# A shorter offset between the first two blocks of a fused attention and mixture-of-experts kernel, with the second block's attention moved into the first three slots

## The chip, the cores and the metric

The kernel runs on one core of a Trainium2 chip. The metric is the device time of one execution in microseconds (us). Three runs of the kernel before took 1556.98, 1557.83 and 1558.25 us; the median is 1557.83 us.

## The reference

Three stages follow one another. The matrices of the second stage come as 64-bit floats; everything else is float32.

```python
# attention: q, k, v are (8, 8, 576, 64); keys and values are averaged over groups of 8
k_p = k.reshape(B, H, Sp, pool, D).mean(axis=3)
v_p = v.reshape(B, H, Sp, pool, D).mean(axis=3)
attn = softmax(scale * np.matmul(q, k_p.transpose(0, 1, 3, 2)))
x = np.matmul(attn, v_p) ...                      # (4608, 512)
# dense layer: w_in is (512, 2048), w_out is (2048, 512)
h = x @ w_in
x = np.maximum(0.01 * h, h) @ w_out
# eight experts, the best one for each token, w1 is (512, 1024), w2 is (1024, 512)
logits = x @ w_gate
out[mask] = gate_w[mask, None] * (np.maximum(x[mask] @ w1[e], 0.0) @ w2[e])
```

## The kernel before, in words

**Precision.** TensorE works on operands split into a high and a low part; a product takes three matmuls (high by high, high by low, low by high). So each weight, each activation and each attention result is first split: ScalarE (ACT) copies the high part, VectorE (DVE) subtracts it to get the low part. Most ACT copies go through the helper `act_copy` (L129) and most DVE subtractions through `sub` (L132), so their lines in the profile are those of the helpers.

**Blocks and slots.** The 4608 tokens are worked on in 18 blocks of 256. The dense layer's 2048 inner columns are 16 pieces `f` of 128. A **slot** is one pair (block b, piece f). Its steps are `g1` (12 matmuls of 128x256 at L498, an ACT copy with factor 0.01, the DVE maximum at L506), `g_hi` and `g_lo` (the split of the result) and, two slots later, `g2` (six matmuls of 128x512 at L526). The list `seq` holds the slots in order. Blocks 0 and 1 are interleaved: block 1 follows block 0 by `LAG` pieces. With `LAG = 4` slots 0 to 3 are pieces 0 to 3 of block 0; then the two blocks alternate; slots 28 to 31 are the last four pieces of block 1. From slot 32 on, one block after the other follows.

**Weights of the dense layer.** In the opening each 64-bit piece of `w_in` (kind 0) and `w_out` (kind 1) must be turned into two float32r parts. `w_conv1` does the first half on a piece: two ACT activations (L463, L464) and four DVE operations (L465, L468, L471, L474). `w_conv2` does the second: an ACT copy and a DVE subtraction. The function `conv` calls them within a slot:

```python
def conv(s, b, f):
    f += LAG * b
    kinds = (b,) if s > LAG and f < NF else (0, 1) if b == 0 else ()
    # w_conv2 for piece f + 1 and w_conv1 for piece f + 2, for each kind in kinds
```

Up to slot `LAG` a slot of block 0 converts both kinds; after that a slot of block 0 converts `w_in` and a slot of block 1 `w_out`. Each slot of block 0 needs its `w_in` piece for `g1`.

**Order of the work.** Every engine executes its own instructions in the order in which the program issues them. Within a slot the loop issues: `g1`; `g_lo` of the slot before; the hooks of this slot (`run_slot`); `g2` of the slot two back; `conv`; `g_hi`. Hooks are functions tied to a slot number by `at(slot, fn, ...)`.

**Attention.** A token tile of 128 rows takes five steps: `att_a` (four TensorE transposes of q at L359, an ACT copy `qT`), `att_b` (eight score matmuls at L378 in two banks; for each bank a DVE maximum at L384 and a subtraction), `att_e` (ACT exponential, L390), `att_n` (DVE row sum, reciprocal and scaling, L394 to L399) and `att_c` (transposes at L410 and L416, ACT copies, DVE subtractions into `at_t` and `rm_t`). When both tiles of a block are through, `att_av` multiplies by the values (16 matmuls at L437 in two banks), and ACT and DVE split the result into the block's input (`x_t`, for block 1 `x1`, printed as `x`). All of these take their PSUM bank from `pt("att")`, which hands out two banks in turn, so a step can start writing only after the step two banks back has been read. Tiles 0 and 1 (block 0) are done ahead of slot 0. Tiles 2 and 3 (block 1) are hooks of slots 0 to 3, and block 1's `att_av` is a hook of slot `LAG`. The hooks of later tiles, of the pooled keys and values of the second sequence (`kvn_k`, `kvn_v`, `kvn_r` at slots 6 to 16) and of the expert weights stand at fixed slot numbers.

Of the kernel before, what the change touches and what calls it, by code (L numbers as in the profile page):

```python
# [21 lines left out]
def kernel(  # L22
# [14 lines left out]
    B, H, S, D = q.shape  # L37
    NT, DM = out.shape
    DFF = moe_w_in.shape[1]
    LAG = 4  # L40
    E, _, FE = moe2_w1.shape
    POOL = 8
    SP = S // POOL
# [953 lines left out]
    seq = []  # L997
    for i in range(NF + LAG):
        if i < NF:
            seq.append((0, i))  # L1000
        if i >= LAG:
            seq.append((1, i - LAG))
    seq += [(b, f) for b in range(2, NB) for f in range(NF)]
# [3 lines left out]
    def at(slot, fn, *a):  # L1007
        hooks.setdefault(slot, []).append((fn, a))

    def plan():  # L1010
        for t in range(4, NT // P):
            b, i = divmod(t, TPB)
            s = (b - 1) * NF + 1 + 7 * i
            at(s - 1, att_a, t)
            if t + 1 < NT // P:
                at(s - 1, q_load, t + 1)
            at(s + 1, att_b, t)
            at(s + 2, att_e, t)
            at(s + 3, att_n, t)
            at(s + 5, att_c, t)  # L1020
        for b in range(2, NB):
            at((b - 1) * NF + NF - 1, att_av, b)
        for nb in range(2, B):
            t = S * nb // P
            b, i = divmod(t, TPB)
            sb_ = (b - 1) * NF + 2 + 7 * i
            use = []
            c = sb_ - 1
            while len(use) < 4:
                if c % NF in (1, 3, 5, 8, 10, 12, 14) and (not use or use[0] - c >= 3):  # L1030
                    use.insert(0, c)
                c -= 1
            use += [use[3] + 2, use[3] + 4, use[3] + 6]
            for i in range(7):
                at(use[i], kv_use, nb, i)
                if i + 2 < 7:
                    at(use[i], kv_load, nb, i + 2)
                at(use[i] - 2 + (i > 3), kv_pool, nb, i)
            at(max(use[0] - 6, 0), kv_load, nb, 0)
            at(use[0] - 5, kv_load, nb, 1)  # L1040
        for i in range(E * NCH):
            s = 34 + i * 9 // 5
            at(s, ps_load, i)
            at(s + 2, ps_split, i)
            at(s + 3, ps_store, i)
        for b in range(NB - 1):
            s = (b + 1) * NF + 1
            lg_at = []
            if b == 0:
                at(30, y_evac, 0)  # L1050
                at(31, y_tr, 0, 0)
                at(32, y_tr, 0, 1)
                at(33, y_logit, 0)
                r = (34, 36)
            elif b == 1:
                ev, r = 37, (46, 48)
                lg_at = [38 + j // 2 for j in range(16)]
            elif b == NB - 2:
                ev, r = None, (s + 9, s + 11)
                lg_at = [s + j // 2 for j in range(16)]  # L1060
            else:
                ev, r = None, (s + 15, s + 19)
                lg_at = [s + max(j - 1, 0) for j in range(16)]
            if b == 1:
                at(ev, y_evac, b)
            for j, x in enumerate(lg_at):
                at(x, logit, b, j)
            at(r[0], route_a, b)
            at(r[1], route_b, b)
            at(r[1], route_c, b, 0)  # L1070
            at(r[1] + 2, route_c, b, 1)
# [34 lines left out]
    with tc.manual_schedule():  # L1106
# [66 lines left out]
            at(6 + 2 * i, kvn_k, 1, i)  # L1173
        at(14, kvn_v, 1)
        at(16, kvn_r, 1)
        for fn, t, o in zip((att_a, att_b, att_e, att_n, att_c) * 2, (2,) * 5 + (3,) * 5, (0, 0, 1, 1, 2, 1, 1, 2, 2, 3)):
            at(o, fn, t)
        at(LAG, att_av, 1)
        at(31, prefill)
        at(36, step_consts)  # L1180
        at(20, lambda: nc.sync.dma_start(out=wgk, in_=moe2_w_gate.rearrange("(k p) e -> p k e", p=P)))
        at(27, gate_rows)
        at(4, q_load, 4)
        plan()
        pend = []
# [4 lines that stand above are left out]
            for kind in kinds:  # L1190
                if (kind, f + 1) in w_mid:
                    w_conv2(kind, f + 1)
                    if w_todo:
                        w_load64()
            for kind in kinds:
                if (kind, f + 2) in w_raw:
                    w_conv1(kind, f + 2)
# [171 lines left out]
```

## Time and profile before

| | |
|---|---|
| median of three runs | 1557.83 us |
| profiled execution, its own time | 1558.05 us |
| its span, first to last instruction | 1556.0 us |
| TensorE matmuls busy (PE) | 1472.8 us, 95% |
| VectorE busy (DVE) | 939.4 us, 60% |
| ScalarE busy (ACT) | 626.8 us, 40% |
| mean granted TensorE clock | 0.975 |

Busy shares are averages over stages with different limits, so a change in one stage has to be read from that stage's own stretch. The opening, slots 0 to 31, lies between about 36 and 197 us of the span. Times in the rows are microseconds from the span's start.

### The profile page before, as it was taken

What the parts mean: (1) busy time and instruction counts of PE and PEld (TensorE: products, weight loads), DVE (VectorE), ACT (ScalarE), POOL (GpSimd) and SP (SyncE); (2) the same over time, 40 slices, a digit from 0 to 9 for tenths busy, and PEclk for the clock granted to TensorE, in tenths of its full rate; (3) what the DMA queues carried; (4) which work ended last, traced back from release to release, by engine and by line L of the source; (5) the groups of instructions that cost most, each with busy time, mean ns of one, the idle gap of its engine ahead of it and who ended that gap; (6) DMA issues with size and microseconds to landing.
All of it is one profiled execution on the core that took longest, in us unless ns stands there. A gap on an engine that the chain in (4) does not pass through costs nothing. (4 is left out here: it accounts for less than half of the span.)

```text
span 1556.0 us, 25769 instructions
## 1 busy us (share of the span) xinstructions
PE 1472.8 (95%) x9272; PEld 1317.6 (85%) x9272; DVE 939.4 (60%) x2468; ACT 626.8 (40%) x1442; POOL 327.3 (21%) x294
## 2 busy tenths in 40 slices
PE   3698989999999999999999999999799999999998
PEld 3586879999898888899989989988699999998887
DVE  6998658879778878877877977664122121211111
ACT  4676434544444454444444444322122222222222
POOL 4000012232232233222222332121212111111111
PEclk8699999999999999999999999999899999999999
DMA  9443135555544545535645644143511117566160
GB/s 216 148 132 100 63 99 190 167 188 169 169 167 166 182 149 185 184 140 171 197 153 157 203 149 163 48 178 122 245 41 55 35 48 300 211 257 259 41 250 24
DMA packets 121386, 238.06 MB, mean 153 GB/s; under 512 B 56845, under 2 KB 65041, under 8 KB 117544
## 3 DMA queue, kind: packets, MB, share of 16 engines
q1 hardware_dynamic: 90312, 139.81, 28.7%
q10 hardware_dynamic: 23328, 76.56, 13.0%
q0 software_dynamic: 7616, 20.01, 3.8%
q8 instruction: 75, 1.23, 0.3%
q14 instruction: 55, 0.45, 0.1%
HBM read 317.78 MB, written 87.38 MB: 260 GB/s over the span
## 5 line engine op out<-in xcount | busy, mean ns | idle before, releaser
L526 PE MATMUL y<-w,ghl 128*128 128x512 f32 x1728 | 466.3, 406 | 2.8 <-DVE ghl L132 2.5
L526 PEld LDWEIGHTS y<-w,ghl 128*128 128x128 f32 x1728 | 310.1, 192 | 61.7 <-DVE ghl L132 6.3
L132 POOL TENSOR_TENSOR ps<-ps 128x512 f32<-128x512 f32 x128 | 181.6, 1419 | 482.2 <-ACT ps L129 361.8
L498 PEld LDWEIGHTS h<-x_t,w 128*128 128x128 f32 x1776 | 239.6, 195 | 39.8 <-DVE w L132 16.9
L498 PE MATMUL h<-x_t,w 128*128 128x256 f32 x1776 | 246.4, 288 | 24.0 <-DVE w L132 15.3
L546 DVE CUSTOM_DVE_ANT_0 junk<-y,wg 128x512 bf16<-128x512 f32 x256 | 200.3, 783 | 1.9
L498 PEld LDWEIGHTS y<-x_t,w 128*128 128x128 f32 x1488 | 193.2, 189 | 9.6
L498 PE MATMUL y<-x_t,w 128*128 128x256 f32 x1488 | 196.1, 282 | 0.0
L935 PE MATMUL y<-w,ghl 128*128 128x512 f32 x672 | 176.5, 401 | 0.9 <-DVE ghl L923 0.9
L935 PEld LDWEIGHTS y<-w,ghl 128*128 128x128 f32 x672 | 120.4, 190 | 22.4 <-DVE ghl L923 1.3
L129 ACT ACTIVATE g<-h 128x256 f32<-128x256 f32 x164 | 63.0, 384 | 145.9 <-PE h L498 132.8
L991 POOL DMA_INDIRECT out_dram<-kv,sidx x40 | 40.1, 1003 | 382.5 <-ACT kv L990 199.3
L923 DVE SCALAR_TENSOR_TENSOR ghl<-h,ghl 128x256 fp32r<-128x256 f32 x56 | 23.8, 425 | 135.9 <-ACT ghl L922 135.9
L506 DVE TENSOR_TENSOR h<-g,h 128x256 f32<-128x256 f32 x132 | 56.0, 424 | 77.7 <-ACT g L129 77.2
L132 DVE TENSOR_TENSOR at_t<-a,at_t 128x512 fp32r<-128x512 f32 x62 | 42.7, 688 | 87.6 <-ACT at_t L129 87.2
L129 ACT ACTIVATE ghl<-h 128x256 fp32r<-128x256 f32 x132 | 50.7, 384 | 92.9 <-PE y L526 42.8
L129 ACT ACTIVATE ps<-ps 128x512 fp32r<-128x512 f32 x128 | 80.5, 629 | 17.8 <-DMA ps<-in_moe_w_dram 8.7
L129 ACT ACTIVATE ghl<-y 128x256 fp32r<-128x256 f32 x124 | 47.3, 382 | 95.2 <-DVE y L506 50.5
L132 DVE TENSOR_TENSOR x_t<-a,x_t 128x512 fp32r<-128x512 f32 x60 | 41.1, 688 | 51.7 <-ACT x_t L129 51.7
L129 ACT ACTIVATE g<-y 128x256 f32<-128x256 f32 x124 | 47.4, 382 | 60.9 <-PE y L498 53.4
L295 DVE TENSOR_TENSOR kv<-kv 72x512 f32<-72x512 f32 (+8 forms) x126 | 68.0, 540 | 3.2
L613 POOL DMA_INDIRECT lst<-ent,six x36 | 37.8, 1051 | 150.4 <-DVE six L612 115.1
(291 smaller groups left out, 2157.2 us busy)
## 6 DMA issues: line engine op xcount, KB each, us to landing
w<-wsp SPq DMA_DIRECT2D x108, 2048.0 KB
wsp<-ps ACTq DMA_DIRECT2D x128, 512.0 KB
ps<-in_moe_w_dram SPq DMA_DIRECT2D x128, 256.0 KB
y_d<-y ACTq DMA_DIRECT2D x18, 512.0 KB
q<-in_q_dram SPq DMA_DIRECT2D x28, 256.0 KB
kv<-in_k_dram SPq DMA_DIRECT2D x24, 288.0 KB
kv<-in_v_dram SPq DMA_DIRECT2D x24, 256.0 KB
ps<-in_moe_w_in_dram SPq DMA_DIRECT2D x8, 512.0 KB
```

Of the source, the lines that this page charges most:

```text
L129: nc.scalar.activation(o, i, AF.Copy, scale=scale)
L132: eng.tensor_tensor(out=o, in0=a, in1=b, op=ALU.subtract)
L295: eng.tensor_tensor(out=o, in0=t[:, :, 0:w], in1=t[:, :, w:2 * w], op=ALU.add)
L498: nc.tensor.matmul(p[:, 0:BLK], win(f)[:, kk, l], xv[:, kk, r], start=(n == 0), stop=(n == 3 * KD - 1))
L506: nc.vector.tensor_tensor(out=g, in0=t, in1=h, op=ALU.max)
L526: nc.tensor.matmul(y_ps[b, i], hl[:, l, i * P:i * P + P], wout(f)[:, r], start=(f == 0 and l + r == 0), stop=(last and l == 1),)
L546: nc.vector.tensor_tensor_reduce(out=jk, in0=y_sb[b][:, i], in1=wg_t[0][:, e], scale=1.0, scalar=0.0, op0=ALU.mult, op1=ALU.add, accum_out ...
L613: nc.gpsimd.indirect_dma_start(out=lst, out_offset=bass.IndirectOffsetOnAxis(ap=ix[:, 0:1], axis=0), in_=ent[:, i, :], in_offset=None, bou ...
L923: nc.vector.scalar_tensor_tensor(out=hl[:, 1], in0=b, scalar=0.0, in1=f32(hl[:, 0]), op0=ALU.max, op1=ALU.subtract)
L935: nc.tensor.matmul(o_ps[2 * p + i], hl[:, l, i * P:i * P + P], w[:, r], start=(f == 0 and l + r == 0), stop=(f == 7 and l == 1),)
L991: nc.gpsimd.indirect_dma_start(out=out, out_offset=bass.IndirectOffsetOnAxis(ap=sidx[:, t:t + 1], axis=0), in_=o, in_offset=None, bounds_c ...
```

## The change

`LAG` becomes 2. Slots 0 to 2 are then pieces 0 to 2 of block 0, the two blocks alternate from slot 3 to slot 28, and slots 29 to 31 are the last pieces of block 1; there are still 32 slots. `conv` converts both kinds in slots 0, 1 and 2 instead of 0 to 4, nothing in slot 3, and one kind per slot from slot 4 on. The attention steps of tiles 2 and 3 and of block 1's `att_av` get new slots. The evacuation and the logits of block 0 move on by one slot each.

```diff
-    LAG = 4
+    LAG = 2
...
             if b == 0:
-                at(30, y_evac, 0)
-                at(31, y_tr, 0, 0)
-                at(32, y_tr, 0, 1)
-                at(33, y_logit, 0)
-                r = (34, 36)
+                at(31, y_evac, 0)
+                at(32, y_tr, 0, 0)
+                at(33, y_tr, 0, 1)
+                at(34, y_logit, 0)
+                r = (35, 37)
...
-        for fn, t, o in zip((att_a, att_b, att_e, att_n, att_c) * 2, (2,) * 5 + (3,) * 5, (0, 0, 1, 1, 2, 1, 1, 2, 2, 3)):
+        for fn, t, o in zip((att_a, att_b, att_e, att_n, att_c) * 2, (2,) * 5 + (3,) * 5, (0, 0, 0, 1, 1, 1, 1, 1, 2, 2)):
             at(o, fn, t)
         at(LAG, att_av, 1)
```

**ACT in slot 0.** `g<-h` is the activation of `g1`, `qT` the query of tile 2, `pr<-pr` its exponential, `w<-ps` and `w<-y` are the high parts of `w_conv2`, the L463 and L464 rows belong to `w_conv1`. Before:

```order
L129 ACTIVATE g<-h_362 128x256
L129 ACTIVATE qT<-a_378 128x512
L129 ACTIVATE w_301<-ps 128x4x128
L129 ACTIVATE w_332<-y_113 128x512
L463 ACTIVATE junk<-r_114 128x512
L464 ACTIVATE e_107<-junk,ebias 128x512
```

and with the change:

```order
L129 ACTIVATE g<-h_362 128x256
L129 ACTIVATE qT<-a_378 128x512
L390 ACTIVATE pr<-pr 128x576
L129 ACTIVATE w_301<-ps 128x4x128
L129 ACTIVATE w_332<-y_113 128x512
L463 ACTIVATE junk<-r_114 128x512
L464 ACTIVATE e_107<-junk,ebias 128x512
```

The exponential of tile 2 has moved from slot 1 to slot 0, ahead of the copies and activations of the weight conversion.

**DVE in slot 1.** Rows L394 to L399 are `att_n` of tile 2, `w_118<-a` are the two banks of `att_b` of tile 3, `w_301<-r_114` is the first subtraction of `w_conv2`. Before:

```order
L394 TENSOR_REDUCE st<-pr 128x8
L395 TENSOR_SCALAR st<-st 128x8
L396 RECIPROCAL st<-st 128x8
L399 TENSOR_TENSOR pn<-pr,st 128x512
L399 TENSOR_TENSOR pn<-pr,st 128x64
L384 TENSOR_REDUCE w_118<-a_447 128x4
L132 TENSOR_TENSOR w_118<-a_447,w_118 128x288
L384 TENSOR_REDUCE w_118<-a_452 128x4
L132 TENSOR_TENSOR w_118<-a_452,w_118 128x288
L132 TENSOR_TENSOR w_301<-r_114,w_301 128x4x128
```

and with the change:

```order
L394 TENSOR_REDUCE st<-pr 128x8
L395 TENSOR_SCALAR st<-st 128x8
L396 RECIPROCAL st<-st 128x8
L399 TENSOR_TENSOR pn<-pr,st 128x512
L399 TENSOR_TENSOR pn<-pr,st 128x64
L132 TENSOR_TENSOR at_t<-a_441,at_t 128x4x128
L132 TENSOR_TENSOR rm_t<-a_448,rm_t 32x2x128
L384 TENSOR_REDUCE w_118<-a_460 128x4
L132 TENSOR_TENSOR w_118<-a_460,w_118 128x288
L384 TENSOR_REDUCE w_118<-a_465 128x4
L132 TENSOR_TENSOR w_118<-a_465,w_118 128x288
L132 TENSOR_TENSOR w_301<-r_114,w_301 128x4x128
```

The two subtractions of `att_c` for tile 2, which use the transposed output of `att_n`, now follow `att_n` at once; before they stood in slot 2.

**DVE in slot 2, with the change.** `w_118` is tile 3, `x_104` the input of block 1:

```order
L399 TENSOR_TENSOR w_118<-w_118 128x512
L399 TENSOR_TENSOR w_118<-w_118 128x64
L132 TENSOR_TENSOR at_t<-a_513,at_t 128x4x128
L132 TENSOR_TENSOR rm_t<-a_520,rm_t 32x2x128
L132 TENSOR_TENSOR x_104<-a_526,x_104 128x2x256
L132 TENSOR_TENSOR x_104<-a_537,x_104 128x2x256
L132 TENSOR_TENSOR w_301<-kv,w_301 128x4x128
```

`att_n`, `att_c` and `att_av` stand one behind the other; before they were in slots 2, 3 and 4 with conversions of weights between them.

## Rows read from the trace of the kernel before

**Rows 1.** The page: busy time and share of the span of each engine, and the granted TensorE clock in 40 equal slices, in tenths.

```profile
PE 1472.8 (95%) x9272; PEld 1317.6 (85%) x9272; DVE 939.4 (60%) x2468; ACT 626.8 (40%) x1442; POOL 327.3 (21%) x294
...
PEclk8699999999999999999999999999899999999999
```

**Rows 2.** Busy time by stretch: the stretch, its length, busy us (and instructions) of PE, weight loads, DVE, ACT, POOL, then the granted clock, DMA share, GB/s. They are slot 1, slot 2, slot 3 and slots 5 to 24, each cut where DVE begins a slot's maximum.

```profile
51.80:62.40 10.60, 6.77 (x27) 5.97 (x27) 10.22 (x23) 6.11 (x12) 0.00 (x0) 0.50 0.29 99
62.40:72.45 10.05, 6.46 (x25) 5.41 (x25) 9.68 (x21) 6.21 (x12) 0.00 (x0) 0.67 0.31 104
...
72.45:80.51 8.06, 5.74 (x37) 4.86 (x36) 7.79 (x15) 5.83 (x10) 0.00 (x0) 0.98 0.51 149
...
88.62:172.04 83.42, 73.32 (x424) 60.53 (x424) 75.69 (x148) 56.07 (x116) 0.69 (x3) 0.94 0.29 89
```

**Rows 3.** Whom DVE waited for between 26 and 172 us: total us, times, longest us.

```profile
DVE e L465 <- ACT e L464: 2.1, 4, 0.6
DVE w L132 <- ACT w L129: 1.4, 3, 0.9
DVE vr L132 <- ACT vr L129: 1.4, 2, 0.9
DVE g L506 <- ACT g L129: 0.5, 1, 0.5
...
```

**Rows 4.** Whom PE waited for between 36 and 197 us, same columns: its largest wait, and that of a transpose for its bank.

```profile
PE h L498 <- DVE w L132: 15.3, 6, 3.9
...
PE a L359 <- DVE at_t L132: 2.3, 1, 2.3
```

**Rows 5.** DVE in order of time, slot 1: start, length, instruction. Slot 1's maximum, att_n's first operation (g_lo lies between), att_b's first, att_b's last operation, the two subtractions of w_conv2; then at_t in slot 2.

```profile
51.80 0.41 DVE L506 TENSOR_TENSOR g<-g,h 128x256 f32<-128x256 f32 x1
...
52.47 0.75 DVE L394 TENSOR_REDUCE st<-pr 128x8 f32<-128x576 f32 x1
...
54.44 0.45 DVE L384 TENSOR_REDUCE w<-a 128x4 f32<-128x288 f32 x1
...
55.78 0.46 DVE L132 TENSOR_TENSOR w<-a,w 128x288 f32<-128x288 f32 x1
56.15 0.68 DVE L132 TENSOR_TENSOR w<-r,w 128x512 fp32r<-128x512 f32 x1
56.75 0.68 DVE L132 TENSOR_TENSOR w<-kv,w 128x512 fp32r<-128x512 f32 x1
...
63.06 0.69 DVE L132 TENSOR_TENSOR at_t<-a,at_t 128x512 fp32r<-128x512 f32 x1
63.78 0.41 DVE L132 TENSOR_TENSOR rm_t<-a,rm_t 32x256 fp32r<-32x256 f32 x1
64.22 0.75 DVE L394 TENSOR_REDUCE w<-w 128x8 f32<-128x576 f32 x1
```

**Rows 6.** ACT in order of time: the exponential of tile 2 and what follows it in slot 1, then a copy of w_conv2 and the two activations of w_conv1 in slot 16.

```profile
49.12 0.68 ACT L390 ACTIVATE pr<-pr 128x576 f32<-128x576 f32 x1
49.70 0.60 ACT L129 ACTIVATE w<-a 128x512 f32<-128x512 f32 x1
...
134.86 0.66 ACT L129 ACTIVATE w<-ps 128x512 fp32r<-128x512 f32 x1
135.42 0.65 ACT L463 ACTIVATE junk<-y 128x512 bf16<-128x512 bf16 x1
136.11 0.72 ACT L464 ACTIVATE e<-junk,ebias 128x512 uint32<-128x512 uint16 x1
```

**Rows 7.** DVE at the same place in slot 16, with the idle time before it in brackets.

```profile
136.87 0.69 DVE L465 SCALAR_TENSOR_TENSOR e<-y,e 128x512 uint32<-128x512 uint32 x1 [0.62 <-ACT e L464]
```

**Rows 8.** Transposes and scores: att_c's four transposes on PE behind att_n, ahead of slot 0, with ACT's copy; the score matmuls of tile 3 in slot 1; the four transposes again in slot 22.

```profile
23.44 1.09 PE L410 MATMUL a<-ident,pn 128*128 128x128 f32 x4 [3.52 <-DVE pn L399]
...
24.56 0.60 ACT L129 ACTIVATE at_t<-a 128x512 fp32r<-128x512 f32 x1 [2.94 <-PE a L410]
...
50.35 2.29 PE L378 MATMUL a<-kT,w 128*128 128x144 f32 x8 [0.69 <-ACT w L129]
...
157.14 0.60 PE L410 MATMUL a<-ident,pn 128*128 128x128 f32 x4
```

**Rows 9.** att_av on PE: first and last rows of the second bank of block 0, ahead of slot 0, and of the first bank of block 1, in slot 4; each bank is 8 matmuls.

```profile
34.09 0.84 PE L437 MATMUL a<-at_t,vm 128*128 128x256 f32 x3
...
35.41 0.28 PE L437 MATMUL a<-rm_t,vr 128*128 128x256 f32 x1
...
76.30 0.52 PE L437 MATMUL a<-at_t,vm 128*128 128x256 f32 x3
...
77.14 0.28 PE L437 MATMUL a<-rm_t,vr 128*128 128x256 f32 x1
```

**Rows 10.** The end of the opening. DVE's subtraction of the last w_in piece, in slot 24; on PE, g1 of slot 24, which came after the 2.3 us wait of rows 4, and of slots 26, 28 and 32.

```profile
171.43 0.69 DVE L132 TENSOR_TENSOR w<-ps,w 128x512 fp32r<-128x512 f32 x1
...
165.65 2.76 PE L498 MATMUL h<-x_t,w 128*128 128x256 f32 x12
...
173.40 1.60 PE L498 MATMUL h<-x_t,w 128*128 128x256 f32 x12
...
179.48 1.57 PE L498 MATMUL h<-x,w 128*128 128x256 f32 x12
...
196.76 1.60 PE L498 MATMUL h<-x_t,w 128*128 128x256 f32 x12
```

## The prediction, made before the changed kernel was run

> **What bounds the kernel now.** The page comes first [rows 1]: PE is busy for 95% of the span and DVE for 60%, which makes TensorE look like the limit. But the clock line starts with 8, 6 and then 9s, so the first slices differ from the rest, and the change lies there. Hence the second view, busy time by stretch [rows 2]. In slot 1 DVE is busy 10.22 of 10.60 us and PE 6.77; in slot 2 it is 9.68 of 10.05 against 6.46. From slot 5 to slot 24 DVE is busy 75.69 of 83.42 us. VectorE is the limit of the opening up to about 172 us, and the work that fills it is the conversion of the 64-bit weights. The third view is who waits for whom. From 26 to 172 us DVE waited for others for 5.4 us in all [rows 3], and nearly all of that lies behind slot 4: ACT and PE are normally a slot ahead of it. PE, on the contrary, waited 15.3 us for weights that DVE had not yet subtracted [rows 4]. Last, the end of the stretch [rows 10]: DVE finishes the subtraction of the last w_in piece at 171.43 + 0.69 = 172.12 us, in slot 24; slot 26's g1, which needs it, starts at 173.40; from there PE works through to block 2 at 196.76.
>
> So two numbers decide: when DVE reaches that last w_in subtraction, and how much PE work is left behind it. An idle PE in slots 0 to 4 costs nothing by itself.
>
> **The change, term by term.** The conversion, the attention steps and the slots are the same in number; their total of DVE work does not change. What changes is where DVE waits.
>
> *Slot 0.* The exponential of tile 2 is put on ACT ahead of the copies of w_conv2. It needs att_b, so it starts when att_b's last DVE operation has ended, 0.46 us after that began, while DVE could go on after 56.15 - 55.78 = 0.37 [rows 5]. The ACT instruction behind the exponential follows after 49.70 - 49.12 = 0.58, and the copy takes 0.66 [rows 6]. DVE's subtraction waits 0.46 + 0.58 + 0.66 - 0.37 = 1.33. ACT then goes on with the second copy (0.56 from start to start), L463 (0.69) and L464 (0.72 to its end), so that L464 ends 0.58 + 0.56 + 0.56 + 0.69 + 0.72 = 3.11 after the exponential began, while DVE, which has two subtractions of 0.60 in between [rows 5], is there at 0.58 + 0.66 + 1.20 = 2.44: 0.67 more. Slot 16 shows the same sequence with one copy, and DVE lost 0.62 at that point [rows 7]. Slot 0: **2.0**.
>
> *Slot 1.* att_c's subtraction into at_t now follows att_n directly: transposes, ACT copy, then DVE again. Ahead of slot 0 the same path took 24.56 - 23.44 = 1.12 to the copy and 0.60 for it [rows 8], with the handoffs 1.75. Then att_a of tile 3 must have the bank that at_t is read from; the trace shows that coupling as PE's wait of 2.3 us [rows 4]. From the start of DVE's at_t: 0.69 for it, 1.09 for four transposes, 0.60 for the ACT copy, half of 2.29 for the scores of one bank [rows 5, 8], some 0.15 for three handoffs, together 3.68; DVE is free after the rm_t subtraction, 64.22 - 63.06 = 1.16 on. So 2.5. Then the exponential of tile 3 stands ahead of the conversion, as in slot 0: 2.0. Slot 1: **6.25**.
>
> *Slot 2.* att_n to at_t of tile 3 again: 1.75. Then att_av: 8 matmuls for the first bank took 35.69 - 34.09 = 1.60 [rows 9], ACT's copy 0.60, a handoff: 2.25. The second bank is 1.60 behind, DVE has 0.60 to do: 1.0. L464 is late behind four copies as before: 0.65. Slot 2: **5.65**.
>
> Together 13.9. These are prices at or near the lower clock level of 1.2 GHz: slot 1 had 0.50 granted and slot 2 0.67 [rows 2]. At full clock the four transposes take 0.60 instead of 1.09 [rows 8] and a bank of att_av 77.42 - 76.30 = 1.12, the second 0.96 behind [rows 9], and the scores of a bank half of their 1.15. Slot 1 is then 1.25 + 1.5 + 2.0 = 4.75 and slot 2 1.25 + 1.75 + 0.35 + 0.65 = 4.0, with slot 0 a total of 10.75. I take 13.9, since the changed slots give PE more waiting per us than these two had. The clock-gate part (Part 1) of the Trainium skill's page "TensorE: Matmul & The Clock Gate" says that the array runs throttled unless its activity releases it, and that a 128-column matmul then takes 107 instead of 56 ns; four of them would differ by 0.2 us, an estimate from that page, where the rows have 0.49; with 0.2 at the three places with four transposes the sum below would be 0.9 lower. By that rule the added waits also keep the array slow; the granted 0.50 of slot 1 agrees.
>
> *Slots 3 to 24.* Slot 3 has no conversion, as slot 5 had none; it keeps that place's gaps. From slot 4 each slot has one conversion, as before from slot 6, at the same cost per slot. The hooks at slots 6 to 16 stay with their gaps: 0.
>
> *DVE work now ahead of the last w_in subtraction.* It moves from slot 24 to slot 26, so two more slots' maximum and g_lo (52.47 - 51.80 = 0.67 each) and att_b of tile 5 in slot 25 (56.15 - 54.44 = 1.71) come first [rows 5]: **+3.05**. The weight loads on SP's queue stay tied to w_conv2, piece by piece; DVE waited for none [rows 3], and none is wanted earlier: 0. The evacuation of block 0 with its store on ACT's queue, and the logits, go one slot on, behind the same PE work: 0.
>
> *PE work behind it.* g1 of the last w_in piece is now in slot 28, not 26: 179.48 - 173.40 = **6.08 less** to do [rows 10]. Before, PE came to it 173.40 - 172.12 = 1.28 after the weights were there; now it stands waiting: **-1.28**. While it waits in slot 25, where DVE has an att_b more, its clock may fall; after the similar wait of rows 4 a g1 took 2.76 instead of 1.57 [rows 10]. I take half of that 1.19: **+0.6**.
>
> Sum: 13.9 + 3.05 - 6.08 - 1.28 + 0.6 = **+10.2 us** on the profiled execution's 1558.05, which is 1568.2. That execution is 0.2 above the median of the runs, so **1568.0 us**. Behind slot 32 nothing takes it back: PE is the limit there, at nine tenths or more of the clock [rows 1].
>
> Bounds: all PE prices at full clock and no fall of the clock at the end give 10.75 + 3.05 - 6.08 - 1.28 = +6.4, 1564.2. Above, the clock falls in full (+0.6), att_av runs wholly at 1.2 GHz (twice 1.12 and twice 0.96 in place of 1.60 each, +0.96), and a slow g1 in slot 4 holds DVE's maximum once (+1.2): +13.0, 1570.8.
>
> **The rivals.**
>
> *A. The opening as two regimes that are interleaved better (faster).* PE idles in the first slots and is the limit in the last. If ACT and PE keep their lead over DVE in slots 0 to 2, the added waits vanish and only the end counts: PE has 6.08 less to do behind the last w_in piece, and with 3.05, 1.28 and 0.6 the sum is -3.7, 1554.1. For it speaks that DVE hardly waited in slots 0 to 4 before. Against it: that lead came from a slot of conversion between the steps of attention, and the new order has att_n, at_t, att_b and att_av back to back on DVE. It decides where the waits of slots 0 to 2 together stay under 3.7 us (under 0.6 for a gain that can be measured). The section "Optimization Strategy" under "Identifying Performance Opportunities" of the Trainium skill's page "Perfetto Trace Analysis" says just this: a kernel whose most contended engine changes over time may gain by interleaving the regimes. The trace agrees that there are two regimes, DVE's up to 172 us and PE's behind. Chance 0.06.
>
> *B. A wash.* The waits come to between 0.6 and 6.8 us, because PE and ACT begin att_c's work while DVE is still at something else, and the time stays within 3.1 us of before, about 1558. Rows 5 and the new order leave DVE nothing else to do there. Chance 0.08.
>
> *C. The clock comes up early (slower, but less).* PE's work is denser in slots 0 to 2, and the prices are those at full clock: 1564.2. For it: 0.98 was granted in slot 3; against it: 0.50 in slot 1 [rows 2], with nearly the same PE work. Chance 0.2.
>
> *D. The change does not do what it says,* that is, LAG moves conversions so that another engine than DVE sets the pace in slots 4 to 24. It can't: In slots 5 to 24 PE was busy 73.32 us, its waits for DVE left out, against 75.69 [rows 2], and the order gives both the same slots in the same sequence. If PE did set the pace there, a few tenths of a us in each of 20 slots would come on top, some 1573. Chance 0.02.
>
> **How the numbers follow.** A measurement of this kernel tells about 0.2%, or 3.1 us, from no change. The forecast, waits at the lower clock, has 0.64; C has 0.2; B has 0.08; A has 0.06; D's 0.02 is slower as well. So faster is 0.06, same 0.08 and slower 0.86. The likeliest case is 1568.0, its own range 1564 to 1571. The range for 8 in 10 takes in C and reaches a little to B and above the upper bound for a wait that no row prices: 1561 to 1572.
>
> **What the changed profile would show.** Right: DVE idle of 10 us or more in slots 0 to 2, laid to ACT's at_t, x and w copies, L464 and PE's scores, where DVE had been busy 96%; slot 3's maximum at about 89 us, where before slot 5's began at 88.62; from there the same pace of slots; DVE's last w_in subtraction at about 189 us, and block 2's first g1 at about 207 instead of 196.76, and every later stage shifted by as much. Wrong: DVE busy in slots 0 to 2 as before, or block 2's g1 before 197 us (then A), a granted clock near 1.00 in slots 1 and 2 with idle near 10.75 (C), or a new wait behind slot 4 or a loss behind 207 us, which nothing here prices.

## The result and the profile after

The changed kernel takes **1569.84 us** (median of four runs, 1566.24 to 1570.15) against 1557.40 us before (four runs, 1555.7 to 1558.25): a ratio of 1.0076, with a 95% interval of 1.0058 to 1.0093. It is slower by 12 us. Forecast were 1568.0 us, a range of 1561 to 1572, and a chance of 0.86 for slower. The profiled execution took 1570.15 us, its span is 1568.0.

The page hardly differs from [rows 1]: busy time and instructions, then the granted clock in 40 slices.

```profile
PE 1476.1 (94%) x9272; PEld 1318.9 (84%) x9272; DVE 940.0 (60%) x2468; ACT 625.2 (40%) x1442; POOL 327.4 (21%) x294
...
PEclk8599999999999999999999999999899999999999
```

DVE's work has not grown (939.4 before, 940.0 now), and the instructions are as many as before. Busy time by stretch, the columns as in [rows 2], for slots 0, 1 and 2 and for 94.6 to 162 us:

```profile
42.80:53.20 10.40, 3.30 (x13) 2.71 (x12) 8.25 (x17) 5.06 (x9) 0.00 (x0) 0.50 0.60 200
53.20:71.70 18.50, 8.14 (x30) 6.36 (x30) 11.64 (x25) 6.90 (x13) 0.00 (x0) 0.59 0.17 57
71.70:88.90 17.20, 12.35 (x62) 10.68 (x62) 11.17 (x23) 6.81 (x13) 0.00 (x0) 0.71 0.25 75
94.60:162.00 67.40, 59.84 (x349) 47.97 (x347) 61.46 (x121) 46.17 (x95) 0.00 (x0) 0.97 0.40 122
```

DVE was busy for 10.22 of 10.60 us in slot 1 before; now it is busy for 11.64 of 18.50, and in slot 2 for 11.17 of 17.20. From slot 5 on it is at nine tenths again. The granted clock of slots 1 and 2 was 0.50 and 0.67 before and is 0.59 and 0.71, so TensorE, for which DVE waits directly or by way of ACT, still works at or near its 1.2 GHz level there: 0.50 from 54 to 64 us and again from 71.7 to 79 us, where the transposes and the scores run. DVE in order of time shows the single waits; these are its instructions with an idle time before them (in brackets, with who ended it), the maximum of slot 3, and the subtraction of the last w_in piece:

```profile
46.24 0.69 DVE L132 TENSOR_TENSOR w<-ps,w 128x512 fp32r<-128x512 f32 x1 [1.29 <-ACT w L129]
...
48.12 0.69 DVE L465 SCALAR_TENSOR_TENSOR e<-r,e 128x512 uint32<-128x512 uint32 x1 [0.58 <-ACT e L464]
...
57.64 0.69 DVE L132 TENSOR_TENSOR at_t<-a,at_t 128x512 fp32r<-128x512 f32 x1 [1.76 <-ACT at_t L129]
...
61.55 0.46 DVE L384 TENSOR_REDUCE w<-a 128x4 f32<-128x288 f32 x1 [2.77 <-PE a L378]
...
64.76 0.69 DVE L132 TENSOR_TENSOR w<-r,w 128x512 fp32r<-128x512 f32 x1 [1.30 <-ACT w L129]
...
66.65 0.69 DVE L465 SCALAR_TENSOR_TENSOR e<-kv,e 128x512 uint32<-128x512 uint32 x1 [0.60 <-ACT e L464]
...
76.18 0.69 DVE L132 TENSOR_TENSOR at_t<-a,at_t 128x512 fp32r<-128x512 f32 x1 [1.76 <-ACT at_t L129]
...
79.66 0.69 DVE L132 TENSOR_TENSOR x<-a,x 128x512 fp32r<-128x512 f32 x1 [2.35 <-ACT x L129]
81.37 0.69 DVE L132 TENSOR_TENSOR x<-a,x 128x512 fp32r<-128x512 f32 x1 [1.01 <-ACT x L129]
...
83.83 0.69 DVE L465 SCALAR_TENSOR_TENSOR e<-ps,e 128x512 uint32<-128x512 uint32 x1 [0.56 <-ACT e L464]
...
88.87 0.41 DVE L506 TENSOR_TENSOR g<-g,h 128x256 f32<-128x256 f32 x1
...
188.09 0.68 DVE L132 TENSOR_TENSOR w<-ps,w 128x512 fp32r<-128x512 f32 x1
```

The brackets add up to 1.87 us in slot 0, 6.43 in slot 1 and 5.68 in slot 2: 13.98 where 13.9 was forecast, each at the place that the working named. PE in order of time, from g1 of slot 28, which needs the last w_in piece, to g1 of slots 32 to 35 and 39; L1101 is the logits of block 0:

```profile
188.80 1.59 PE L498 MATMUL h<-x_t,w 128*128 128x256 f32 x12
...
205.65 1.59 PE L498 MATMUL h<-x_t,w 128*128 128x256 f32 x12
...
209.37 1.60 PE L498 MATMUL h<-x_t,w 128*128 128x256 f32 x12
...
212.29 1.70 PE L498 MATMUL h<-x_t,w 128*128 128x256 f32 x12 [0.89 <-DVE ghl L132]
213.82 1.14 PE L378 MATMUL a<-kT,qT 128*128 128x144 f32 x8
215.87 1.92 PE L1101 MATMUL a<-wgk,kv 128*128 128x8 f32 x16 [0.90 <-DVE pr L132]
217.65 2.44 PE L526 MATMUL y<-w,ghl 128*128 128x512 f32 x6
219.88 2.36 PE L498 MATMUL h<-x_t,w 128*128 128x256 f32 x12
...
239.52 1.60 PE L498 MATMUL h<-x_t,w 128*128 128x256 f32 x12
```

and in the kernel before g2 of slot 34 and g1 of slots 35 and 39:

```profile
206.01 1.64 PE L526 MATMUL y<-w,ghl 128*128 128x512 f32 x6
207.49 1.60 PE L498 MATMUL h<-x_t,w 128*128 128x256 f32 x12
...
227.03 1.59 PE L498 MATMUL h<-x_t,w 128*128 128x256 f32 x12
```

Block 2's first g1 starts at 205.65, 8.89 us later than in [rows 10]. This execution began slot 0 0.70 us earlier (maximum at 42.82, before 43.52), so the opening cost 9.59. Behind it stands a loss that no term of the forecast priced, in slot 34: the score matmuls (L378) of a later tile and the logits now share that slot, the logits wait for DVE to read the scores out of their bank, and the next g2 and g1 take 2.44 and 2.36 us instead of 1.64 and 1.60, at a granted clock of 0.61 (217.7 to 222.1 us). From slot 32 to slot 39 the kernel took 30.27 us before (196.76 to 227.03) and takes 33.87 (205.65 to 239.52): **3.6 us**. From there the two traces stay 12.5 to 12.6 us apart to beyond 600 us.

### The profile page after: what moved, and what is told of

The parts are those of the page before. It is cut to its first block, busy times and chain, and to the rows that moved or that the text cites. A ratio compares the mean times of both kernels' runs of the same rounds, so it can differ in the third digit from the quotient of the medians.

```text
span 1568.0 us, 25778 instructions
## 1 busy us (share of the span) xinstructions
PE 1476.1 (94%) x9272; PEld 1318.9 (84%) x9272; DVE 940.0 (60%) x2468; ACT 625.2 (40%) x1442; POOL 327.4 (21%) x294
## 5 line engine op out<-in xcount | busy, mean ns | idle before, releaser
L132 DVE TENSOR_TENSOR ghl<-h,ghl 128x256 fp32r<-128x256 f32 x132 | 55.5, 421 | 23.6 <-ACT ghl L129 22.6
```

The lines of the kernel that those rows point to most:

```text
L132: eng.tensor_tensor(out=o, in0=a, in1=b, op=ALU.subtract)
```

## The experiments

**Theory 1**: the loss is DVE's waits in slots 0 to 2, made by where the attention steps stand and not by the offset; a smaller part comes from the logits in slot 34. **Theory 2**: the shorter offset itself costs the time, whatever DVE waits for there.

### Attention alone

The kernel before with `LAG = 4` and the attention steps where the change puts them:

```diff
-(2,) * 5 + (3,) * 5, (0, 0, 1, 1, 2, 1, 1, 2, 2, 3)):
+(2,) * 5 + (3,) * 5, (0, 0, 0, 1, 1, 1, 1, 1, 2, 2)):
...
-        at(LAG, att_av, 1)
+        at(2, att_av, 1)
```

> The kernel before (LAG 4), with only the attention steps of tiles 2 and 3 in the change's slots and att_av of block 1 in slot 2. Theory 1: the same waits of DVE, 14.0 us in slots 0 to 2, and nothing gained at the end; less the 1.3 us by which PE came late to the last weights, +12.7, about 1570. Theory 2 (the offset itself costs): within 2 us of before, about 1557.

Measured: 1570.08 us (1567.77 to 1571.55), a ratio to before of 1.0086 (1.0065 to 1.0106). Whom DVE waited for between 36 and 92 us (total us, times, longest):

```profile
DVE at_t L132 <- ACT at_t L129: 3.5, 2, 1.8
DVE x L132 <- ACT x L129: 3.4, 2, 2.4
DVE w L384 <- PE a L378: 2.8, 1, 2.8
DVE w L132 <- ACT w L129: 2.6, 2, 1.3
...
```

These are the waits of the changed kernel, without its offset, and a loss of the same size is there, so theory 2 is out. It is made up otherwise: block 2 starts at 210.99 us, 14.23 later than in the kernel before, and slots 32 to 39 take 29.50 us. The changed kernel loses less up to block 2 (8.89, the difference being what its offset gives) and 3.6 more behind it.

### The exponentials one slot later

The changed kernel; `att_e` of tiles 2 and 3 comes one slot after the `att_b` that it needs, as in the kernel before, so that ACT need not wait for DVE's `att_b` ahead of the copies of `w_conv2`:

```diff
-(0, 0, 0, 1, 1, 1, 1, 1, 2, 2)
+(0, 0, 1, 1, 1, 1, 1, 2, 2, 2)
```

> The changed kernel (LAG 2), with the exponentials of tiles 2 and 3 issued one slot later (in slots 1 and 2), as they were before. Theory 1 (DVE's waits behind ACT and PE in slots 0 to 2 make the loss): the waits for the w copies and L464 in slots 0 and 1, 1.29 + 0.58 and 1.30 + 0.60 in the changed kernel's profile, go and the time falls by 3.8 us, to about 1566. Theory 2 (the shorter offset itself costs, wherever the attention stands): no change, about 1570.

Measured: 1566.40 us (1565.47 to 1569.48), ratio 1.0074 (1.0052 to 1.0096). In the same view the w copies are gone and the rest stands:

```profile
DVE at_t L132 <- ACT at_t L129: 3.5, 2, 1.8
DVE x L132 <- ACT x L129: 3.0, 2, 2.3
DVE w L384 <- PE a L378: 2.8, 1, 2.8
DVE e L465 <- ACT e L464: 1.3, 3, 0.5
...
```

From slot 0's maximum to slot 3's it is 41.55 us (43.59 to 85.14) instead of 46.05. The two waits of PE in slot 34 are as in the changed kernel, but the clock did not fall behind them (it was granted in full, 1.00, from 212.3 to 217.1 us):

```profile
208.78 1.70 PE L498 MATMUL h<-x_t,w 128*128 128x256 f32 x12 [0.89 <-DVE ghl L132]
...
212.36 1.92 PE L1101 MATMUL a<-wgk,kv 128*128 128x8 f32 x16 [0.90 <-DVE pr L132]
214.13 1.63 PE L526 MATMUL y<-w,ghl 128*128 128x512 f32 x6
215.60 1.60 PE L498 MATMUL h<-x_t,w 128*128 128x256 f32 x12
```

Slots 32 to 39 take 32.24 us here (202.15 to 234.39), 1.63 less than in the changed kernel. So the same two waits can go with a fall of the clock or without one; what decides it is open.

### The logits back in slot 33

The changed kernel, with these hooks as before the change:

```diff
-                at(33, y_tr, 0, 1)
-                at(34, y_logit, 0)
-                r = (35, 37)
+                at(32, y_tr, 0, 1)
+                at(33, y_logit, 0)
+                r = (34, 36)
```

> The changed kernel, with the two transposes of block 0's result both in slot 32 and its logits in slot 33, the routing in 34 and 36, as it was before; attention as in the change. Theory 1a (3.6 us of the loss come from slot 34, where the logits now share the slot with att_b of tile 6 and PE waits twice and then runs at the lower clock): slot 35's g1 comes at +9 against before instead of +12.4, and the time falls by 3 to 3.6 us, to about 1566.5. Rival (the later g_lo rule, or the delay itself, makes that loss): it stays within 1 us of the changed kernel, about 1570.

Measured: 1564.47 us (1562.27 to 1567.95), ratio 1.0062 (1.0041 to 1.0083). Its g1 of slots 32, 34, 35 and 39:

```profile
206.24 1.60 PE L498 MATMUL h<-x_t,w 128*128 128x256 f32 x12
...
213.97 1.67 PE L498 MATMUL h<-x_t,w 128*128 128x256 f32 x12
217.85 1.59 PE L498 MATMUL h<-x_t,w 128*128 128x256 f32 x12
...
235.92 1.59 PE L498 MATMUL h<-x_t,w 128*128 128x256 f32 x12
```

Block 2 starts where it did (206.24), and slots 32 to 39 take 29.68 us instead of 33.87. The collision in slot 34 is shown as the second part of the loss; the 1.2 us that the median gained beyond it lie within the spread of the runs. By their ratios to the kernel before, this experiment and the last gained less than by their medians (1.0062 and 1.0074, from 1.0076), and the intervals overlap. So the sizes of single steps rest on the traces and not on the times.

### Attention without the waits

If theory 1 holds, the offset of 2 must cost nothing once DVE has other work at each of these places. First with the early steps ahead of slot 0, around the second `w_conv1` pair (prologue and hooks of the changed kernel replaced):

```diff
+        att_a(2)
         w_conv1(0, 1)
+        att_b(2)
         w_conv1(1, 1)
+        att_a(3)
+        att_e(2)
+        att_b(3)
...
+        for o, fn, t in ((0, att_e, 3), (0, att_n, 2), (0, att_n, 3), (0, att_c, 2), (1, att_c, 3)):
```

> The changed kernel (LAG 2), with the attention of tiles 2 and 3 spread so that on DVE no step stands right behind the one it needs: att_a, att_b and one exponential ahead of slot 0 between the conversions of weights, att_n of both tiles and att_c of tile 2 in slot 0, att_c of tile 3 in slot 1, att_av in slot 2. Theory 1: 12 to 13 of the 14.0 us of waits go, the loss in slot 34 stays: 1557 to 1558, no change against before. Theory 2: the loss stays, 1568 to 1570.

Measured: 1558.74 us (1550.61 to 1565.86), ratio 1.0007 (0.9983 to 1.0031). Two long waits are left in the opening, 1.49 us for L464 and 2.03 for the maximum of slot 0, and slots 32 to 39 still take 34.06. With the logits in slot 33 as above:

> LAG 2 with the attention spread as in the run before it and the logits of block 0 back in slot 33. Theory 1 and 1a (the loss is DVE's waits in slots 0 to 2 plus the loss in slot 34, and the two add): the spread took 11 us back, the logits alone 3 to 4; together 1554 to 1556, a little under before. Rival (the two losses overlap, or a shorter offset costs by itself): 1558 or more.

Measured: 1556.08 us (1552.99 to 1559.24), ratio 0.9993 (0.9978 to 1.0007); slots 32 to 39 take 29.71. Then the two remaining waits were filled, by steps placed so that DVE has a conversion or a step of the other tile between two steps of one tile (again against the changed kernel, the logits in slot 33):

```diff
         w_conv1(0, 1)
+        att_a(2)
         w_conv1(1, 1)
+        att_b(2)
...
+            (0, att_e, 2), (0, att_a, 3), (0, att_n, 2), (0, att_b, 3), (0, att_e, 3), (0, att_n, 3), (0, att_c, 2),
+            (1, att_c, 3),
```

> As the run before, with the attention of tiles 2 and 3 placed so that two of the three remaining waits of DVE (1.49 us for L464 ahead of slot 0, 2.03 us for g1 of slot 0 behind tile 3's scores) go, at the price of about 1.1 us for the exponentials in slot 0. Theory 1: 2 to 2.5 us less, 1552 to 1554. Rival (what is left of the waits no longer decides, PE does): no change.

Measured: 1553.24 us (1551.0 to 1562.59), ratio 0.9970 (0.9949 to 0.9992). Block 2 starts at 193.59 us.

### Some of DVE's work on GpSimd

Here DVE's work itself, not a wait, is the suspect. In the kernel before, the `w_out` subtractions go to GpSimd (POOL):

```diff
-        sub(nc.vector, dl, w, f32(dh))
+        sub(nc.gpsimd if kind and f > 0 else nc.vector, dl, w, f32(dh))
```

> The kernel before (LAG 4), with the subtraction of the low part of the w_out pieces 1 to 15 on GpSimd, which is idle in this stretch, in place of DVE. Theory 1 (DVE sets the pace up to slot 24): 14 subtractions of 0.60 us leave DVE's path ahead of the last w_in piece, 8.4 us; PE takes over as the limit in the slots with kvn_k (7.24 us of PE work a pair against 7.57 - 0.60 of DVE), and it came 1.3 us late to the last piece, so 5 to 7 us less, about 1551. Rival (ACT, PE or the loads set the pace, or GpSimd slows DVE by as much as it saves): within 2 us of before.

Measured: 1559.13 us (1557.66 to 1563.34), ratio 1.0015 (1.0002 to 1.0029): a miss. DVE and POOL in order of time:

```profile
96.06 0.43 DVE L468 TENSOR_SCALAR ps<-ps 128x512 uint32<-128x512 uint32 x1
...
99.92 1.52 DVE L468 TENSOR_SCALAR ps<-ps 128x512 uint32<-128x512 uint32 x1
```

```profile
99.84 1.32 POOL L132 TENSOR_TENSOR w<-ps,w 128x512 fp32r<-128x512 f32 x1 [5.63 <-DVE e L465]
```

The same DVE instruction takes 0.43 us alone and 1.52 beside the subtraction; it ends 0.28 us behind it (99.84 + 1.32 = 101.16, and 101.44). Three of the moved subtractions fall beside this instruction: each saved DVE some 0.60 us and cost it 1.09. Of all fourteen ahead of the last w_in piece, the ten behind 80 us cost a DVE instruction 0.9 to 1.1 us and the four before them 0 to 0.6, so DVE's last w_in subtraction starts at 175.02 instead of 171.43. The section "SBUF: two separate sides" of the Trainium skill's page "SBUF — State Buffer" says that GpSimd and some of DVE's instructions share one pair of ports under an exclusive lock, and that whoever comes second is blocked until the other's instruction ends. The two rows agree with it. The same edit on the kernel of the last section:

> Both: LAG 2 with the second spread, logits in slot 33, and the w_out subtractions on GpSimd. Theory 1: the gains add as far as DVE stays the limit; with two slots less of PE work behind the last weight, 5 to 7 us under the second spread, 1546 to 1548. Rival: PE is the limit by now and little comes on top of the better of the two.

Measured: 1559.82 us (1557.88 to 1565.47), ratio 1.0011 (0.9993 to 1.0029); the last w_in subtraction starts at 180.74 instead of 176.03 and block 2 at 198.30 instead of 193.59, 4.71 later both. A second miss, by the same cause: here too three of the L468 beside a subtraction take 1.51 to 1.53 us.

### DVE work out of the way of the last w_in piece

The kernel with the logits in slot 33 and the waits filled, and tile 5's attention two slots later (`att_c` one), behind the conversions:

```diff
+            d = 2 if t == 5 else 0
-            at(s - 1, att_a, t)
+            at(s - 1 + d, att_a, t)
...
-        at(27, gate_rows)
+        at(28, gate_rows)
```

> The second spread, with the steps of tile 5 two slots later (att_c one), so that att_b of tile 5 no longer stands on DVE ahead of the last w_in subtraction. Theory 1 (each us of DVE on that path counts): 1.71 less there, 1551 to 1552. Rival (PE is the limit by then): no change, 1553.

Measured: 1552.33 us (1548.56 to 1556.05), ratio 0.9971 (0.9954 to 0.9989); block 2 starts at 193.01. DVE's last w_in subtraction comes 1.87 us earlier (174.16 instead of 176.03), as expected, but from the g1 that needs it to block 2 PE now takes 18.15 us instead of 16.86, so that block 2 comes only 0.58 earlier; in the times the step can't be told from noise. Then also the second half of the pooled values (`kvn_r`) in slot 17 instead of 16:

```diff
-        v_rest(nb % 2, f)
+        kvn[2] = f
...
+        at(17, lambda: v_rest(1, kvn[2]))
```

> As the run before, with the second half of kvn_r (the four ACT copies and the two DVE subtractions into vr) one slot later, in slot 17, so that DVE does not stand behind its own output by way of ACT: it waited 0.48 + 0.88 + 0.88 + 0.62 = 2.9 us there in every kernel so far. Theory 1: a wait of this kind costs the same wherever DVE is the limit, 2 to 2.9 less, about 1549. Rival: the wait moves to slot 17, no change.

Measured: **1549.40 us** (1543.96 to 1555.48), ratio 0.9942 (0.9917 to 0.9968): faster than both kernels, and than the kernel before by 0.6%. Block 2 starts at 190.05, 2.96 earlier, and the waits at `kvn_r` that the expectation named are gone from the trace. In the first slots, between 26 and 92 us, all that DVE still waits for is:

```profile
DVE e L465 <- ACT e L464: 0.9, 2, 0.5
DVE w L394 <- ACT w L390: 0.7, 1, 0.7
DVE g L506 <- ACT g L129: 0.5, 1, 0.5
DVE st L394 <- ACT pr L390: 0.4, 1, 0.4
```

### The offset alone

The best kernel with an offset of 4 again:

```diff
-    LAG = 2
+    LAG = 4
...
-                at(31, y_evac, 0)
-                at(32, y_tr, 0, 0)
+                at(30, y_evac, 0)
+                at(31, y_tr, 0, 0)
...
-        at(LAG, att_av, 1)
+        at(2, att_av, 1)
```

> As the run before, with LAG back at 4 (evacuation and transposes of block 0 in the slots of the kernel before, att_av of block 1 in slot 2): the same attention without the shorter offset. Theory 1: the offset by itself is worth 6.08 us of PE behind the last w_in piece less two slots' maximum and g_lo on DVE, 1.34, so this is 3 to 5 us slower than the run before, 1552 to 1554. Rival (the offset is worth nothing, all gain came from the spread): the same as the run before.

Measured: 1558.26 us (1553.23 to 1562.82), ratio 1.0006 (0.9987 to 1.0025). So the offset of 2 is worth 8.9 us between the medians, more than the 3 to 5 that were expected. DVE's last w_in subtraction and block 2's first g1, first with the offset of 2:

```profile
171.24 0.68 DVE L132 TENSOR_TENSOR w<-ps,w 128x512 fp32r<-128x512 f32 x1
...
190.05 1.60 PE L498 MATMUL h<-x_t,w 128*128 128x256 f32 x12
```

and with 4:

```profile
170.64 0.68 DVE L132 TENSOR_TENSOR w<-ps,w 128x512 fp32r<-128x512 f32 x1
...
196.24 1.60 PE L498 MATMUL h<-x_t,w 128*128 128x256 f32 x12
```

DVE is done at the same time within 0.6 us, and those are the start of slot 0 (45.43 and 44.86): the two more maxima and `g_lo` that the offset of 2 puts ahead of it (1.3) are balanced by longer waits with the offset of 4 (L464 2.3 us instead of 1.5 up to 172 us, the w copies 0.6 instead of 0.3). PE then has 25.60 us of work to block 2 instead of 18.81. That makes 6.19 us at block 2, and 6.22 at 377 us. The other 2.7 between the medians lie within the spread of the runs. The two profiled executions are 9.65 apart: the distance of their traces falls to 4.9 at 433 us and rises to 8.9 between 634 and 683, most of it where PE waits between 640 and 660 us. Busy time there, columns as in [rows 2], offset 4 and then offset 2:

```profile
640.00:660.00 20.00, 17.82 (x110) 15.82 (x110) 18.19 (x49) 9.37 (x25) 6.02 (x5) 0.91 0.53 168
```

```profile
640.00:660.00 20.00, 20.00 (x134) 18.26 (x133) 17.40 (x53) 10.18 (x26) 8.38 (x7) 1.00 0.70 160
```

With the offset of 4 PE idles for 2.2 us and the clock falls, as it does in the kernel before in the same stretch (PE busy 17.82, clock 0.91); with 2 neither happens. How a shift of the opening decides on that is open.

## Why the prediction was right

**The limit and the place.** Right. DVE paces the opening, PE the end of it; the time went where DVE waited. One reading was short: DVE's waits from 26 to 172 us were 5.8 us in all and not 5.4, the first four lines of [rows 3]; nothing in the sum hangs on it.

**The waits of slots 0 to 2.** Right in place, releaser and size: 2.0, 6.25 and 5.65 forecast, 1.87, 6.43 and 5.68 measured. The single prices held too: the copy behind the exponential 1.33 and measured 1.29, at_t 1.75 and 1.76 twice, the bank of the scores 2.5 and 2.77, att_av 2.25 + 1.0 and 2.35 + 1.01. The choice of the prices at the lower clock held: the granted clock of slots 0 and 1 was 0.50 and 0.59, and the full-clock total of 10.75 would have missed by 3.2.

**DVE work ahead of the last w_in piece, +3.05.** Right within 0.4. From slot 0's maximum to that subtraction it is 145.27 us (before 127.91), 17.36 more; 13.98 of it are the waits, 3.38 the rest. In the experiment with the offset alone this path is equally long with both offsets (125.81 us with 2, 125.78 with 4), with 1.14 us less of waits at 2; that leaves 1.2 for the two slots, where 1.34 was forecast.

**PE work behind it, -6.08, and PE no longer late, -1.28.** Right: g1 of slot 28 starts at 188.80, 0.03 us behind the subtraction. From there to block 2 it is 16.85 us, where rows 10 had 17.28 from slot 28. The difference of 0.43 was not in the sum; a group of block 0's transposes has moved from slot 31 to slot 32, behind the measured point. The experiment with the offset alone shows the term as 25.60 - 18.81 = 6.79; this includes these transposes and the scores of tile 5 (L378, 1.14 us), which stand behind the last w_in piece with the offset of 4 there and ahead of it with 2.

**The fall of the clock at the end, +0.6.** It did not come. PE waited 2.02 us just ahead of slot 28 and g1 took 1.59, at a granted clock of 1.00; after the similar wait of [rows 4] it took 2.76.

**Evacuation and logits of block 0, 0.** This is the step that failed, a cost put at nothing. The working said "one slot on, behind the same PE work: 0" and looked at the PE work only. Slot 34 has `att_b` of a later tile, both steps take banks in turn from the same pair, and so the logits wait for DVE's reads. Measured 3.6 us, of which 1.5 are longer waits of PE (6.0 instead of 4.5 for slots 32 to 39) and 1.6 one g2 and one g1 at a lower clock (2.44 and 2.36 instead of 1.64 and 1.60); 0.5 is not assigned. With the logits back in slot 33 the loss was gone (29.68), and with the clock staying up it was 1.63 smaller (32.24). It was this "loss behind 207 us, which nothing here prices" that the text named as a sign of error.

**The sum.** 10.2 forecast; 9.59 + 3.6 = 13.2 measured from slot 0 to slot 39, 0.7 less for the earlier start of slot 0, and 0.4 given back later: 12.1 between the profiled executions. "Behind slot 32 nothing takes it back" holds in the balance and not in the parts: the distance of the two traces is 12.5 at 377 us, 9.7 at 702 and 11.6 at 862. That the time lies only 1.8 us from the forecast is therefore in part luck: 3.6 us were missed, and 2.1 went the other way (0.6 of clock, 0.4 of transposes, 0.7 of the start, 0.4 later).

**The rivals.** A, the interleaving that wins, failed here for the reason given: the waits of slots 0 to 2 were 14 and not under 3.7. But it was right on what the offset can give: with the waits filled the same offset is worth 6.2 us in the opening and 8.9 between the medians, and the best kernel takes 1549.4. The rule on interleaving regimes that was cited there, from the section "Optimization Strategy" of the Trainium skill's page "Perfetto Trace Analysis", says that such a kernel may gain; the trace of that kernel agrees, with a ratio of 0.9942 at the offset of 2 against 1.0006 at 4. B needed waits under 6.8 and C the full-clock prices, and neither came. D needed a slower pace in slots 4 to 24, and that pace did not change (the slots without attention are 3.79 us apart, as before).

## What to carry to other kernels

On an in-order engine that is the limit, count for each moved step what the engine has to do between an operation and the one that needs its result by way of two other engines: a step put directly behind the one it depends on costs the whole round trip, here 1.8 us for a transpose and 2.4 for a product. A moved step must be priced against what its new slot already holds in shared buffers (two banks in turn), not only against the work of one engine. And a change that loses may hold a half that wins: the offset and the placement had to be tried apart to see that the offset took 6.2 us off the opening (8.9 between the medians) and the placement added 13.

## What the runs showed of the hardware

A DVE instruction with one operand in and one out, 0.43 us alone, took 1.52 us beside a GpSimd subtraction of 1.32 us; the work moved off DVE cost it more than it saved (the last w_in subtraction at 175.02 instead of 171.43). Waits of PE of the same length (0.89 and 0.90 us) were followed by the lower clock in one kernel and not in another, and one of 2.02 us by none, so a wait's length alone did not tell whether the clock falls.
